# A full-width last query tile, joint first scores, a scale from a sum of squares, and constant matmuls in planned waits

## The chip, the cores and the metric

The kernel runs on one core of one Trainium2 chip. What is measured is the device time of one execution in microseconds (us). The kernel before was run three times; one more execution was taken with a profile.

## The reference

An attention layer with a memory term feeds two dense blocks, one after the other. B = 4 batches, H = 8 heads, S = 576 positions, D = 64; the model width is 512, the hidden width 2048, and there are 2304 tokens. All inputs are f32.

```python
scores = where(causal, -1e9, (q @ k.T) / sqrt(D))
a = exp(scores - scores.max(-1)); a /= a.sum(-1) + 1e-9
local = a @ v
q_p = phi(q)                       # phi(x) = where(x > 0, x, exp(x) - 1) + 1
mem_out = (q_p @ M_prev) / (q_p @ z_prev + 1e-6)
g = sigmoid(beta)                  # one per head
x = g * mem_out + (1 - g) * local  # then [tokens, 512]
h = x @ w_in;  x = (h * sigmoid(h)) @ w_out            # first layer
h = x @ w_in2; y = (h * tanh(softplus(h))) @ w_out2    # second layer
```

## The kernel before

**Attention.** Heads are worked in 16 pairs, one head on partitions 0 to 63 and one on 64 to 127. Each pair is visited twice (`VISITS`): the first 16 visits do query tiles 0 and 1 (128 queries each), the next 16 do tiles 2, 3 and 4. Tile 4 has only 64 queries, as 576 = 4 x 128 + 64. A step is one tile of one visit (`STEPS`), 80 in all. `stage_a` makes the scores of a step into PSUM, takes the row maximum on VectorE (L580), the exponential on ScalarE, a high and a low f16 half, and transposes both by DMA. `stage_b`, three steps later, multiplies the transposed halves with V and the memory matrices, and divides. `stage_c` transposes the result on TensorE (L645) and stores it.

The scores of tiles 0 and 1 contract over 64 rows, one head at a time, in f32, each tile as an operation of its own: four records on 64 rows, then two mask matmuls on 128. For tile 4 both heads stand side by side as 128 columns of a block-diagonal operand (`q4s`, high and low); the products with V take 64 of those columns for each head, into PSUM partitions 0 to 63, so their stationary operand is 128 x 64, and the following transpose works on 64 rows.

**The two layers.** Tokens are worked in nine chunks of 256 (`TOK`), first all chunks through layer one, then through layer two. `gemm1` and `gemm2` are the matmuls, on f16 halves; the second layer does them by a scheme of seven products. `chunk_x` loads a chunk, finds a power of two to scale it by, and makes the halves. The scale comes from `largest`: the row maxima go onto a diagonal (`diag`), an f32 matmul with a constant spreads them over all partitions, and VectorE takes the maximum. `weight_scale` uses `largest` too, twice for each layer. The first layer's weights are put together from two 32-bit words on ScalarE and VectorE while they are loaded (`weight_unit`, VectorE's share at L357); the second layer's are read during attention, put together and written back (`weight_single`, to `wd`), and read again later (`weight_pair`).

**The order.** Everything is handed to a planner (`Plan`) with a priority, a choice of engines, an estimated duration, and the regions it writes and reads. `issue` then plays the work through against these estimates, engine by engine, and emits each instruction at its place; each engine runs its instructions in that order. Attention's priorities grow by `A_RATE` = 2.3 a step, so attention and the first layer's matmuls share TensorE. Until a planned time of 50 us (`COLD`) the estimates of TensorE are doubled. In `mm` a matmul's estimate comes from its columns, its type and its rows.

All operations go through a few helpers, so many rows carry a helper's line: L409 every matmul, L349 every activation, L354, L357 and L363 VectorE's tensor-scalar, scalar-tensor-tensor and tensor-tensor (L363 GpSimd's too), L419 every plain DMA.

Of the kernel before, what the change touches and what calls it, by code (L numbers as in the profile page):

```python
# [9 lines left out]
F32 = mybir.dt.float32  # L10
# [24 lines left out]
COLD = 50000.  # L35
XMAX = 8.0
WMAX = ((128.0, 2048.0), (4.0, 64.0))
# [21 lines left out]
class Plan:  # L59
# [6 lines left out]
    def __init__(self):  # L66
        self.ops, self.seen, self.shared = [], {}, set()

    @staticmethod
    def region(a):  # L70
        if isinstance(a, tuple):
            return a
        ap = a.ap
        size = SIZE[a.dtype]
        p0, f0 = divmod(a.offset, ap[0][0])
        f1 = f0 + sum(st * (n - 1) for st, n in ap[1:]) + 1
        name = a.tensor.name
        return (name, p0, p0 + ap[0][1], f0 * size, f1 * size)

    def add(self, prio, choices, writes, reads, tail=0, edge=(0, 0), shared=False):  # L80


        k, deps = len(self.ops), set()
        for regs, w in ((reads, False), (writes, True)):
            for r in map(self.region, regs):
# [12 lines left out]
        if shared:  # L98
            self.shared.add(k)
        return k  # L100
# [4 lines left out]
    def issue(self):  # L105
# [10 lines left out]
        moved, stream = 0.0, 0.0  # L116
# [13 lines left out]
        for _ in range(n):  # L130
# [56 lines left out]
def attn_moe_moe2_kernel(ctx: ExitStack, tc: tile.TileContext, kq, vm, beta, w1, w2, out):  # L187
# [45 lines left out]
    gb, = buf("gb", [H], F32)  # L233
    gv, = buf("gv", [H // 2, 4], F32)
    eps, = buf("eps", [4], F32)
# [27 lines left out]
    diagr, mxr = ring(buf("diag", [128], F32, 2)), ring(buf("mx", [4], F32, 4))  # L263
# [9 lines left out]
    arenas = {F32R: buf("arena_r", [3584], F32R)[0], F32: buf("arena", [18432], F32)[0]}  # L273
# [23 lines left out]
    q1r, q2r, q4s = ring(carve([256], F32, 2)), ring(carve([2, 256], F32R, 2)), carve([2, D], F32R, 2)  # L297
# [3 lines left out]
    scr, topr, scaler, gvr = ring(scales), ring(carve([2], BF16, 3)), ring(carve([1], F32, 3)), ring(carve([4], F32, 3))  # L301
    er_ = ring(carve([S], F32, 2))
    pr, phr = ring(carve([1024], F32, 2)), ring(carve([16, 128], F16, 3))
# [93 lines left out]
    def mm(prio, ms, whole=False):  # L397

        ns, edge = 0, None
        for o, l, r, _, _ in ms:  # L400
            n = cols(o)
            load, more = (107, 58) if r.dtype == F32 else (107, 42) if r.dtype == F32R else (14, 2.5)
            one = max((2 if r.dtype == F32 else 1) * n / 2.4 * l.shape[0] / 128 + more, 30)
            ns += one
            edge = (edge or (load, 0))[0], one

        def go():
            for o, l, r, a, z in ms:
                nc.tensor.matmul(out=o, lhsT=l, rhs=r, start=a, stop=z)  # L409

        writes = [m[0] for m in ms]
        if whole:
            writes = [(t, 0, 128, b0 // 2048 * 2048, -(-b1 // 2048) * 2048) for t, _, _, b0, b1 in map(plan.region, writes)]
        plan.add(prio, [("PE", ns, go)], writes, [x for m in ms for x in m[1:3]], edge=edge)
# [13 lines left out]
    def setup():  # L428
        p = -1e9
        other(p, "SP", 100, lambda: nc.scalar.dma_start(out=gb, in_=beta), [gb])  # L430
        for x, t in enumerate(q4s):
            for r, e in ((slice(0, 64), 1), (slice(64, 128), 0)):
                o = t[r, e].bitcast(F32)
                plan.add(p + x, [
                    ("DVE", 0.52 * cols(o) + 68, lambda o=o: nc.vector.memset(o, 0.0)),
                    ("POOL", 1.0 * cols(o) + 60, lambda o=o: nc.gpsimd.memset(o, 0.0))], [t[r]], [])

        def consts():
            make_identity(nc, ident16)
            nc.gpsimd.memset(mask, 0.0)  # L440

            for r, c, n in ((slice(0, 128), 0, 128), (slice(0, 64), 128, D), (slice(64, 128), 128, D)):
                m = mask[r, c:c + n]
                nc.gpsimd.affine_select(
                    out=m, in_=m, compare_op=ALU.is_ge, fill=-1e9, base=0, pattern=[[-1, n]], channel_multiplier=1)
            make_identity(nc, ident)
            nc.gpsimd.memset(eps[:, 0:2], 1e-9 * PSCALE)
            nc.gpsimd.memset(eps[:, 2:4], 1e-6)
            nc.gpsimd.memset(ones, 1.0)
            nc.gpsimd.memset(onesf, 1 / XMAX)  # L450
# [5 lines left out]
        other(p, "POOL", 2000, consts, [ident16, mask, ident, eps, ones, onesf, *scales, *v1s])  # L456
# [28 lines left out]
    def prep_q(v, j, prio):  # L485
# [6 lines left out]
        src, q2 = rq[v][:, 256:512], q2r()  # L492
        qq[v, 1] = q2[:, 0], q2[:, 1]
# [14 lines left out]
    def prep_v(v, prio):  # L508
# [6 lines left out]
        total = bank[7][:, 400:401]  # L515
# [22 lines left out]
    def stage_a(n, sbk, prio):  # L538
# [4 lines left out]
        b0 = 512 * sbk[turn[0] % len(sbk)]  # L543
        turn[0] += 1
        ph, P, m1 = phr(), pr(), mr()
        if qt < 4:

            scs = [banks[:, b0 + 512 * e:b0 + 512 * e + N] for e in range(2)]
            ms, nb = [], 4 * nk
# [8 lines left out]
            masks = [(sc[:, N - 128:N], ident16, mask[:, 0:128], False, True) for sc in scs]  # L558
            mm(prio, [x for y in zip(*ms) for x in y] + masks)
            both = banks[:, b0:b0 + 1024].rearrange("p (e c) -> p e c", e=2)[:, :, 0:N]  # L560
# [40 lines left out]
    def stage_b(n, prio):  # L601

        v, qt = STEPS[n]
        R = min(128, S - 128 * qt)
# [3 lines left out]
        if qt < 4:  # L608
            pw = pts.pop(n).rearrange("p (s e k) q -> p s k e q", s=2, e=2)
        else:  # L610
            pw = pts.pop(n).rearrange("p (s k) (e q) -> p s k e q", s=2, e=2)
        ms = []
        for e in range(2):
            o = vb[0:R, 65 * e:65 * e + 65]
# [6 lines left out]
        mm(prio, ms + [(vb[0:R, 130:260], er[v][:, 128 * qt:128 * qt + R], rm[v], True, True)])  # L621
# [3 lines left out]
        g = banks[0:R, 512 * 6:512 * 8].rearrange("p (b c) -> p b c", b=2)[:, 0:m, 0:260].rearrange("p b (a c) -> p b a c", a=4)  # L625
        den, t4, x = denr()[0:R, 0:m], t4r()[0:R, 0:m], xr()[0:R, 0:m]
        each = lambda y: y[0:R].unsqueeze(1).to_broadcast([R, m, 4])
# [3 lines left out]
        tt(prio, t4, g[:, :, :, 0:D], den.unsqueeze(3).to_broadcast([R, m, 4, D]), ALU.mult)  # L631
        tt(prio, x, t4[:, :, 0:2], t4[:, :, 2:4], ALU.add, ("POOL", "DVE"))
        xts[n] = (x, R)

    def stage_c(n, prio):
# [5 lines left out]
        x, R = xts.pop(n)  # L641
        m = 1 + qt % 2
        for i in range(m):
            x2, o = x[:, i].rearrange("p e d -> p (e d)"), bank[6 + i][:, 260:260 + R]
            plan.add(prio, [("PE", 131, lambda o=o, x2=x2: nc.tensor.transpose(o, x2, ident[0:R, 0:R]))], [o], [x2, ident],  # L645
                     edge=(107, 56))
        b, hp = divmod(p, H // 2)
        if b == 0 and qt < 2:
# [4 lines left out]
        copy(prio, xo.rearrange("p (b c) -> p b c", b=m),  # L653
             banks[:, 512 * 6:512 * 8].rearrange("p (b c) -> p b c", b=2)[:, 0:m, 260:260 + R])
# [4 lines left out]
    def largest(prio, s, top, spot, root=0.0):  # L659
# [7 lines left out]
        o = spot[:, 384:512]  # L667
        mm(prio, [(o, onesf, d, True, True)])
        reduce(prio, m, o, ALU.max, AX)
# [106 lines left out]
    def chunk_x(l, c, prio, spot):  # L776
        r, sc, x, top = xs0, xsc(), (xsets, x7r)[l](), mxr()[:, 0:1]
# [3 lines left out]
        if (l, c) != (0, 0):  # L781
            dma(prio, r, src[:, t0:t0 + TOK].rearrange("(k p) t -> p k t", p=128), reads=[(name, 0, NC, t0, t0 + TOK)])
        reduce(prio, top, r, ALU.max, mybir.AxisListType.XY, True)
        largest(prio, s, top, spot)
# [197 lines left out]
    def inputs(l, c, prio):  # L982

        nonlocal n_att
        if l == 0:
# [5 lines left out]
            for u in range(NU * (c - 1) // TOPS, min(NU, NU * c // TOPS)) if c else ():  # L991
                weight_single(u, att_prio(12 + 3.5 * u))
                if u % (NU // 2) == NU // 2 - 1:
                    weight_scale(1, u // (NU // 2), MOE, bank[7])
        xs_of[l, c] = chunk_x(l, c, prio, bank[0] if (l, c) == (0, 0) else bank[7])
# [87 lines left out]
```

## Time and profile before

| what | us |
|---|---|
| three runs, median | 955.02 |
| lowest and highest of them | 950.59, 956.07 |
| profiled execution, whole time | 952.23 |
| its span (first to last instruction) | 950.1 |
| TensorE busy in it | 905.0 |
| VectorE, ScalarE, GpSimd busy | 726.8, 616.4, 400.1 |

The span is what the trace covers; the whole time of that execution is 2.1 us more. Times in the trace count from the start of the span. A busy engine is one with an instruction in flight; matmuls overlap each other, so their price is read from the distance between starts, not from their durations. In the trace an f32 matmul that takes two passes stands as two records.

### The profile page before, as it was taken

Reading aid. Unit: us, or ns where it says so; the run is one execution under the profiler, and the core shown is the slowest. Engines: PE = TensorE matmul, PEld = TensorE weight load, DVE = VectorE, ACT = ScalarE, POOL = GpSimd, SP = SyncE. Lnnn points to the kernel's source line nnn. Section 1 sums busy time; section 2 is a strip of 40 time slices with the busy share of each in tenths; the row PEclk is TensorE's granted clock in tenths of the full one; section 3 lists DMA queues with packets and bytes.
Section 4 is the critical chain, followed back from the end, with each engine's and each line's share of the span. In section 5 each row is a group of like instructions: output and inputs, shape, how many; then the busy total and the mean of one; then the engine's idle time right before and its main releaser. Section 6 shows DMA issues by size and latency. Waiting matters only on the chain.

```text
span 950.1 us, 25452 instructions
## 1 busy us (share of the span) xinstructions
PE 905.0 (95%) x10436; PEld 796.3 (84%) x10436; DVE 726.8 (76%) x1532; ACT 616.4 (65%) x1075; POOL 400.1 (42%) x574
## 2 busy tenths in 40 slices
PE   4569899999999999999999999999999999999997
PEld 3448688888788788788888888999999999999996
DVE  5697876787887877878769756767887888878875
ACT  6889978897787776766655555554555545555553
POOL 1103302342433254324236758254554636635552
PEclk9759899999999999999999999999999999999999
DMA  8978879899699498397453253510010010010010
GB/s 257 316 194 251 193 210 231 257 269 255 177 270 260 139 251 196 85 210 164 101 140 122 90 201 111 178 46 23 25 46 24 23 47 23 25 46 13 13 24 23
DMA packets 155155, 131.29 MB, mean 138 GB/s; under 512 B 111776, under 2 KB 138912, under 8 KB 150944
## 3 DMA queue, kind: packets, MB, share of 16 engines
q1 hardware_dynamic: 154896, 129.68, 51.9%
q8 instruction: 81, 1.33, 0.6%
q14 instruction: 34, 0.28, 0.1%
q10 hardware_dynamic: 144, 0.00, 0.0%
HBM read 77.75 MB, written 25.69 MB: 109 GB/s over the span
## 4 chain that ended last, share of the span: by engine, by line
PE 55%; DVE 1%; ACT 1%; issue 1%; DMA 0%; POOL 0%; ACTq 0%; DVEq 0%
PE banks L409 55%; DVE arena L357 0%; ACT arena L349 0%; PE banks L645 0%; DVE ws L357 0%; ACT w L349 0%; DVE arena L363 0%; DMA yd<-w 0%; POOL g L363 0%; DVE diag L354 0%; DVE mx L366 0%; ACT g L349 0%; ACT ga L349 0%; DVE ga L357 0%; DVE w L357 0%
## 5 line engine op out<-in xcount | busy, mean ns | idle before, releaser
L409 PEld LDWEIGHTS <-w 128*128 128x128 f16 (+1 forms) x3584 | 344.8, 99 | 70.3 <-DVE w L357 23.4
L409 PE MATMUL banks<-arena 128*128 128x128 f16 (+6 forms) x4752 | 292.8, 222 | 6.2 <-ACT arena L349 4.5
L409 PEld LDWEIGHTS <-arena 128*128 128x128 f16 (+1 forms) x4464 | 231.8, 100 | 9.0 <-issue 4.6
L409 PE MATMUL banks<-xh,w 128*128 128x256 f16 x1728 | 210.9, 274 | 4.4 <-DVE xh L357 2.8
L409 PE MATMUL banks<-g,w 128*128 128x256 f16 x1728 | 209.7, 273 | 2.7 <-DVE w L357 1.4
L409 PE MATMUL banks<-w,g 128*128 128x256 f16 x1512 | 181.7, 273 | 0.0
L409 PEld LDWEIGHTS <-g 128*128 128x128 f16 x1512 | 143.9, 98 | 15.2 <-DVE g L357 0.2
L363 POOL TENSOR_TENSOR g<-ga,g 128x512 f16<-128x512 f32 x72 | 98.5, 1371 | 112.3 <-ACT g L349 108.0
L357 DVE SCALAR_TENSOR_TENSOR arena<-arena 128x256 f16<-128x256 f32 (+6 forms) x144 | 112.5, 789 | 11.2 <-ACT arena L349 11.0
L363 POOL TENSOR_TENSOR arena<-arena 128x256 f32<-128x256 f32 x72 | 64.8, 907 | 132.7 <-DVE arena L363 113.1
L349 ACT ACTIVATE arena<-arena 128x256 f32<-128x256 f32 (+6 forms) x184 | 105.0, 593 | 20.6 <-PE banks L409 15.8
L363 POOL TENSOR_TENSOR xh<-xh 128x128 f32<-128x128 f32 x142 | 72.7, 532 | 87.7 <-ACT xh L349 85.8
L363 POOL TENSOR_TENSOR w<-w 128x128 f32<-128x128 f32 x144 | 79.7, 575 | 64.5 <-ACT w L349 62.4
L349 ACT ACTIVATE arena<-banks,arena 128x128 f32<-128x128 f32 (+4 forms) x144 | 73.7, 546 | 32.0 <-DVE arena L580 23.8
L580 DVE TENSOR_REDUCE arena<-banks 128x2 f32<-128x256 f32 (+3 forms) x80 | 64.2, 803 | 24.9 <-PE banks L409 22.1
L349 ACT ACTIVATE ga<-banks,xsc 128x512 f32<-128x512 f32 x72 | 49.4, 686 | 48.7 <-PE banks L409 48.2
L349 ACT ACTIVATE w<-banks 128x128 f32<-128x128 f32 x72 | 19.7, 273 | 82.3 <-PE banks L409 82.3
L357 DVE SCALAR_TENSOR_TENSOR ga<-ga,banks 128x512 f32<-128x512 f32 x72 | 49.0, 680 | 28.2 <-ACT ga L349 27.8
L357 DVE SCALAR_TENSOR_TENSOR g<-w,xsc,g 128x384 f16<-128x384 f32 (+1 forms) x72 | 54.9, 770 | 17.2 <-ACT g L349 16.8
L357 DVE SCALAR_TENSOR_TENSOR g<-xh,xsc,g 128x384 f16<-128x384 f32 (+1 forms) x72 | 56.4, 786 | 10.1 <-ACT g L349 9.1
L349 ACT ACTIVATE g<-ga 128x512 f16<-128x512 f32 x72 | 45.2, 628 | 18.6 <-DVE ga L357 18.2
L349 ACT ACTIVATE g<-w,xsc 128x384 f16<-128x384 f32 (+1 forms) x72 | 46.5, 661 | 8.5 <-POOL w L363 8.0
(117 smaller groups left out, 1108.6 us busy)
## 6 DMA issues: line engine op xcount, KB each, us to landing
ws<-w SPq DMA_DIRECT2D x22, 1024.0 KB, 6.7
arena<-kq SPq DMA_DIRECT2D x16, 576.0 KB, 4.8
w<-w SPq DMA_DIRECT2D x8, 1024.0 KB, 7.7
wd<-w SPq DMA_DIRECT2D x16, 512.0 KB, 3.9
arena<-vm SPq DMA_DIRECT2D x16, 325.0 KB, 4.0
yd<-w SPq DMA_DIRECT2D x36, 128.0 KB, 3.3
ws<-wd SPq DMA_DIRECT2D x9, 512.0 KB, 3.9
xs<-yd SPq DMA_DIRECT2D x9, 512.0 KB, 3.8
```

The lines of the kernel that those rows point to most:

```text
L349: return ("ACT", ns, lambda: nc.scalar.activation(out=out, in_=in_, func=func, scale=scale, bias=bias))
L357: return ("DVE", 1.04 * cols(out) + 160 - over[0], lambda: nc.vector.scalar_tensor_tensor(out=out, in0=in0, scalar=s, in1=in1, op0=op0, op ...
L363: return (e, ns, lambda: eng.tensor_tensor(out=out, in0=in0, in1=in1, op=op))
L409: nc.tensor.matmul(out=o, lhsT=l, rhs=r, start=a, stop=z)
L580: other(prio, "DVE", 1.04 * cols(both) + 70, lambda: nc.vector.tensor_reduce(out=m1, in_=both, axis=AX, op=ALU.max, negate=True), [m1], [b ...
```

## The change

- **Last query tile.** The queries of tile 4 are scaled with those of tiles 2 and 3 and then copied into two masked halves: `own` holds 1 on the partitions of a head and 0 elsewhere. In `stage_b` the products with V take all 128 columns (both heads) for each head's V, into 128 partitions; a masked phi (`e4r`) and a masked gate (`g4`) cancel the halves that belong to the other head. The transpose becomes 128 x 128, and the two 64-column halves of its result are added. The masked copies, the phi, the gate and the sum may go to GpSimd or VectorE.
- **Joint first scores.** Step 0 of a visit makes the scores of tiles 0 and 1 in one TensorE operation, into one pair of banks: tile 0 in columns 0 to 127, tile 1 in columns 128 to 383. All 64-row matmuls come first, then all four masks. Step 1 makes no scores of its own.
- **Scale from a sum of squares.** In `chunk_x` the squares of the row maxima (bf16) are summed over the partitions by one bf16 matmul with ones, one column; the scale is a power of two near `XNORM` over the root of the sum. `weight_scale` of the second layer keeps the diagonal, in two halves in banks 6 and 7.
- **Planner.** New estimates for f32 and two-pass matmuls and for partial rows or columns, and 94 ns for each change of array shape. `regions` tells strided accesses apart where one region covered them before. After a planned time of 70 us (`FILL_FROM`), each time in which the plan has TensorE waiting is filled to six tenths with matmuls of constants, one for each 28 ns, into 60 unused columns of bank 7.
- **Smaller.** `weight_single` gets the priority of 12 attention steps later. The clearing of `q4s` is gone, small buffers moved.

```diff
     def issue(self):
...
-                    ns += max(0, self.ops[k][4][0] - stream)
-                    stream = self.ops[k][4][1]
+                    edge = self.ops[k][4]
+                    ns += max(0, edge[0] - stream) + 94 * (edge[2] != kind)
+                    stream, kind = edge[1], edge[3]
+                    if t > FILL_FROM:
+                        for _ in range(int((t - busy) * FILL_PART / FILL_NS)):
+                            self.fill()
+                    busy = t + ns
...
+        plan.fill = lambda: nc.tensor.matmul(out=bank[7][:, 452:512], lhsT=ident16, rhs=mask[:, 0:60], start=True, stop=True)
...
-        for e in range(2):
-            r = slice(64 * e, 64 * e + 64)
-            src, hi, lo = rq[v][r, 512:576], q4s[0][r, e], q4s[1][r, e]
-            copy(prio, hi, src, 0.125)
-            stt(prio, lo, src, 0.125, hi, ALU.mult, ALU.subtract)
+        for i in range(2):
+            tt(prio, q4s[i], q2[:, i, 256:320].bitcast(F32).unsqueeze(1).to_broadcast([128, 2, D]),
+               own[:, 0:2].unsqueeze(2).to_broadcast([128, 2, D]), ALU.mult, ("POOL", "DVE"))
...
-                if qt < 2:
-                    ms.append([(sc, qq[v, 0][r, c], rk[v][r, 0:N], True, False)])
-                else:
+                if qt == 0:
+                    late = banks[:, b0 + 512 * e + 128:b0 + 512 * e + 384]
+                    ms.append([(sc, qq[v, 0][r, 0:128], rk[v][r, 0:128], True, False),
+                               (late, qq[v, 0][r, 128:256], rk[v][r, 0:256], False, False)])
+                    masks = masks + [late]
+                elif qt > 1:
...
-            pw = pts.pop(n).rearrange("p (s k) (e q) -> p s k e q", s=2, e=2)
+            pw = pts.pop(n).rearrange("p (s k) q -> p s k q", s=2).unsqueeze(3).to_broadcast([128, 2, nk, 2, 128])
...
-        mm(prio, ms + [(vb[0:R, 130:260], er[v][:, 128 * qt:128 * qt + R], rm[v], True, True)])
+        if qt < 4:
+            f = er[v][:, 128 * qt:128 * qt + 128]
+        else:
+            f, g4 = e4r(), gvr()
+            tt(prio, f.rearrange("p (e q) -> p e q", e=2), er[v][:, 512:576].unsqueeze(1).to_broadcast([128, 2, D]),
+               own[:, 0:2].unsqueeze(2).to_broadcast([128, 2, D]), ALU.mult, ("POOL", "DVE"))
+            tt(prio, g4, gvv, own, ALU.mult, ("POOL", "DVE"))
+            gvv = g4
+        mm(prio, ms + [(vb[:, 130:260], f, rm[v], True, True)])
...
+            xw = xwr()
+            copy(prio, xw, bank[6][:, 260:388])
+            tt(prio, xo, xw[:, 0:R], xw[:, R:2 * R], ALU.add, ("POOL", "DVE"))
...
-        largest(prio, s, top, spot)
+        tt(prio, t16, top, top, ALU.mult)
+        mm(prio, [(spot, ones, t16, True, True)])
+        ts(prio, p, spot, 1e-36, ALU.max)
+        inverse(prio, s, p)
+        ts(prio, s.bitcast(U32), s.bitcast(U32), 1, ALU.logical_shift_right, 0x7F800000, ALU.bitwise_and)
+        ts(prio, s, s, 2.0**64 * XNORM, ALU.mult)
...
-                weight_single(u, att_prio(12 + 3.5 * u))
+                weight_single(u, att_prio(24 + 3.5 * u))
```

## Rows read from the trace of the kernel before

**Rows 1.** The chain that ended last: start us, us, what.

```profile
582.49 360.87 PE banks L409 x4774
```

**Rows 2.** Busy us of each engine by stretch, instructions, clock, DMA share, GB/s.

```profile
core 0: us, PE busy (x) PEld busy (x) DVE busy (x) ACT busy (x) POOL busy (x), PEclk, DMA share, GB/s
0.00:75.00 75.00, 44.51 (x327) 31.55 (x328) 52.09 (x125) 58.59 (x103) 9.61 (x33) 0.77 0.91 258
...
100.00:110.00 10.00, 7.50 (x48) 4.73 (x45) 8.07 (x26) 8.08 (x17) 1.47 (x3) 0.66 1.19 237
110.00:300.00 190.00, 187.68 (x1979) 157.96 (x1980) 149.98 (x306) 154.31 (x278) 61.98 (x63) 1.00 0.94 232
300.00:500.00 200.00, 197.18 (x2284) 166.36 (x2281) 154.60 (x308) 137.44 (x246) 75.65 (x88) 1.00 0.70 167
500.00:600.00 100.00, 99.37 (x913) 88.65 (x911) 70.54 (x77) 56.69 (x67) 66.62 (x64) 1.00 0.42 140
600.00:943.00 343.00, 343.00 (x4615) 324.78 (x4613) 266.89 (x647) 177.01 (x324) 173.23 (x314) 1.00 0.10 33
```

**Rows 3.** Timeline of TensorE, 100 to 112 us; in brackets the idle time before.

```profile
103.80 1.03 PE L409 MATMUL banks<-w 128*128 128x128 bf16 x8 [1.99 <-DVE w L357]
...
110.93 1.05 PE L409 MATMUL banks<-g,w 128*128 128x256 f16 x8 [1.36 <-DVE w L357]
```

**Rows 4.** Timeline of TensorE, 111 to 117 us; neighbours alike in names are merged.

```profile
111.92 0.65 PE L409 MATMUL banks<-arena 128*128 128x65 f16 x8
112.41 0.27 PE L645 MATMUL banks<-ident,arena 128*128 128x128 f32 x1
112.52 2.46 PE L409 MATMUL banks<-g,w 128*128 128x256 f16 x21
114.81 0.83 PE L409 MATMUL banks<-arena 128*128 128x65 f16 x14
115.47 1.15 PE L409 MATMUL banks<-g,w 128*128 128x256 f16 x9
116.55 0.49 PE L409 MATMUL banks<-arena 64*128 64x128 f32 x4
```

**Rows 5.** Timeline of TensorE, 300 to 324 us.

```profile
300.39 1.15 PE L409 MATMUL banks<-xh,w 128*128 128x256 f16 x9
301.47 1.39 PE L409 MATMUL banks<-arena 128*64 128x65 f16 x32
302.79 2.79 PE L409 MATMUL banks<-xh,w 128*128 128x256 f16 x24
...
320.05 0.39 PE L409 MATMUL banks<-diag,onesf 128*128 128x128 f32 x2
320.28 0.82 PE L409 MATMUL banks<-g,w 128*128 128x256 f16 x6
320.93 0.17 PE L409 MATMUL banks<-arena,ones 128*128 128x1 bf16 x1
320.96 0.49 PE L409 MATMUL banks<-g,w 128*128 128x256 f16 x3
...
322.72 0.27 PE L645 MATMUL banks<-ident,arena 64*128 64x64 f32 x1 [0.16 <-ACT arena L349]
322.93 1.16 PE L409 MATMUL banks<-g,w 128*128 128x256 f16 x9
```

**Rows 6.** TensorE's groups by form from 110 us on: busy us, mean ns.

```profile
L409 PE MATMUL banks<-diag,onesf 128*128 128x128 f32 x38 | 7.4, 278 | 0.2 <-DVE diag L354 0.2
...
L409 PE MATMUL banks<-arena 64*128 64x128 f32 x24 | 3.0, 322 | 0.0
```

**Rows 7.** DMA issues on the tile `wd`: duration ns, first and last start us.

```profile
L419 SPq DMA_DIRECT2D wd<-w x16: 319/386/1107, 126.5 to 353.6; - x16
...
L419 SPq DMA_DIRECT2D arena<-wd x7: 319/320/402, 484.6 to 580.6; - x7
```

**Rows 8.** Timeline of VectorE, 441 to 450 us.

```profile
444.73 1.37 DVE L363 TENSOR_TENSOR arena<-arena 128x8 f32<-128x8 f32 x1
```

**Rows 9.** Timeline of GpSimd, 441 to 450 us.

```profile
444.01 2.07 POOL L363 TENSOR_TENSOR arena_r<-arena,arena_r 128x576 fp32r<-128x576 f32 x1 [1.71 <-ACT arena_r L349]
```

More of the change, by code (lines that the diff above doesn't have):

```diff
@@ L66, in __init__, with regions @@
     def __init__(self):
-        self.ops, self.seen, self.shared = [], {}, set()
+        self.ops, self.seen, self.shared, self.fill = [], {}, set(), None
     @staticmethod
-    def region(a):
+    def regions(a):
         if isinstance(a, tuple):
-            return a
+            return [a]
         ap = a.ap
@@ L75, in region, with add @@
         p0, f0 = divmod(a.offset, ap[0][0])
[L76 to L80, printed above, removed]
+        (step, count), inner = ap[1], 1 + sum(st * (n - 1) for st, n in ap[2:])
+        if count > 4 or inner >= step:
+            step, count, inner = 0, 1, inner + step * (count - 1)
+        return [(a.tensor.name, p0, p0 + ap[0][1], (f0 + step * i) * size, (f0 + step * i + inner) * size) for i in range(count)]
+    def add(self, prio, choices, writes, reads, tail=0, edge=(0, 0, (False, False), (False, False)), shared=False):
         k, deps = len(self.ops), set()
         for regs, w in ((reads, False), (writes, True)):
-            for r in map(self.region, regs):
+            for r in [y for x in regs for y in self.regions(x)]:
                 log = self.seen.setdefault(r[0], [])
@@ L115, in issue @@
         at, on, end = [0.0] * n, [None] * n, [0.0] * n
-        moved, stream = 0.0, 0.0
+        moved, stream, kind, busy = 0.0, 0.0, (False, False), 0.0
         port = {"DVE": 0.0, "POOL": 0.0}
@@ L269, in attn_moe_moe2_kernel @@
     gram = [bank[i][:, 0:128] for i in range(2)]
-    arenas = {F32R: buf("arena_r", [3584], F32R)[0], F32: buf("arena", [18432], F32)[0]}
+    arenas = {F32R: buf("arena_r", [3840], F32R)[0], F32: buf("arena", [18432], F32)[0]}
     pos = dict.fromkeys(arenas, 0)
@@ L300, in attn_moe_moe2_kernel @@
     scales = carve([4], F32, 3)
-    scr, topr, scaler, gvr = ring(scales), ring(carve([2], BF16, 3)), ring(carve([1], F32, 3)), ring(carve([4], F32, 3))
+    scr, topr, scaler, gvr = ring(scales), ring(carve([2], BF16, 3)), ring(carve([1], F32, 3)), ring(carve([4], F32, 4))
     er_ = ring(carve([S], F32, 2))
+    (gb,), (gv,), (eps,) = carve([H], F32), carve([H // 2, 4], F32), carve([4], F32)
+    own, e4r, xwr = carve([4], F32)[0], ring(carve([128], F32, 2)), ring(carve([128], F32, 2))
     pr, phr = ring(carve([1024], F32, 2)), ring(carve([16, 128], F16, 3))
@@ L397, in mm @@
     def mm(prio, ms, whole=False):
-        ns, edge = 0, None
+        ns, edge, kind = 0, None, None
         for o, l, r, _, _ in ms:
-            n = cols(o)
-            load, more = (107, 58) if r.dtype == F32 else (107, 42) if r.dtype == F32R else (14, 2.5)
-            one = max((2 if r.dtype == F32 else 1) * n / 2.4 * l.shape[0] / 128 + more, 30)
+            n, half = cols(o), l.shape[0] < 128
+            if r.dtype == F32:
+                load, one = 107, 2 * max(n / 1.2 * (0.5 if half else 1) + 3, 55 if half else 111)
+            elif r.dtype == F32R:
+                load, one = 107, n / 4.8 + 6 if half else n / 2.4 + 48
+            else:
+                load, one = 14, max(n / 2.4 * (0.5 if half else 1) + 2.5, 29)
+            now = half, cols(l) < 128
+            if kind not in (None, now):
+                ns += 94
+            kind = now
             ns += one
-            edge = (edge or (load, 0))[0], one
+            edge = (*(edge or (load, 0, now))[0:1], one, *(edge or (load, 0, now))[2:3], now)
         def go():
@@ L412, in mm @@
         if whole:
-            writes = [(t, 0, 128, b0 // 2048 * 2048, -(-b1 // 2048) * 2048) for t, _, _, b0, b1 in map(plan.region, writes)]
+            writes = [(t, 0, 128, b0 // 2048 * 2048, -(-b1 // 2048) * 2048) for x in writes for t, _, _, b0, b1 in plan.regions(x)]
         plan.add(prio, [("PE", ns, go)], writes, [x for m in ms for x in m[1:3]], edge=edge)
@@ L449, in consts @@
             nc.gpsimd.memset(ones, 1.0)
+            nc.gpsimd.memset(own, 0.0)
+            for e in range(2):
+                nc.gpsimd.memset(own[64 * e:64 * e + 64, e:4:2], 1.0)
             nc.gpsimd.memset(onesf, 1 / XMAX)
@@ L454, in consts @@
                 nc.gpsimd.memset(t[:, :, :, D:D + 1], 1.0)
-        other(p, "POOL", 2000, consts, [ident16, mask, ident, eps, ones, onesf, *scales, *v1s])
+        plan.fill = lambda: nc.tensor.matmul(out=bank[7][:, 452:512], lhsT=ident16, rhs=mask[:, 0:60], start=True, stop=True)
+        other(p, "POOL", 2000, consts, [ident16, mask, ident, eps, ones, onesf, own, *scales, *v1s])
         act(p, gb, gb, AF.Tanh, 0.5)
@@ L557, in stage_a @@
                                (sc, ql[r, c], kh[r, 0:N], False, False)])
-            masks = [(sc[:, N - 128:N], ident16, mask[:, 0:128], False, True) for sc in scs]
-            mm(prio, [x for y in zip(*ms) for x in y] + masks)
-            both = banks[:, b0:b0 + 1024].rearrange("p (e c) -> p e c", e=2)[:, :, 0:N]
+            masks = [(sc[:, cols(sc) - 128:], ident16, mask[:, 0:128], False, qt > 1 or i > 1) for i, sc in enumerate(masks)]
+            if qt != 1:
+                mm(prio, [x for y in zip(*ms) for x in y] + masks)
+            both = bass.AP(scs[0].tensor, scs[0].offset, [scs[0].ap[0], [512, 2], [1, N]])
             P = P[:, 0:2 * N].rearrange("p (e c) -> p e c", e=2)
@@ L624, in stage_b @@
         m = 1 + qt % 2
-        g = banks[0:R, 512 * 6:512 * 8].rearrange("p (b c) -> p b c", b=2)[:, 0:m, 0:260].rearrange("p b (a c) -> p b a c", a=4)
-        den, t4, x = denr()[0:R, 0:m], t4r()[0:R, 0:m], xr()[0:R, 0:m]
-        each = lambda y: y[0:R].unsqueeze(1).to_broadcast([R, m, 4])
+        g = banks[:, 512 * 6:512 * 8].rearrange("p (b c) -> p b c", b=2)[:, 0:m, 0:260].rearrange("p b (a c) -> p b a c", a=4)
+        den, t4, x = denr()[:, 0:m], t4r()[:, 0:m], xr()[:, 0:m]
+        each = lambda y: y.unsqueeze(1).to_broadcast([128, m, 4])
         tt(prio, den, g[:, :, :, D], each(eps), ALU.add)
@@ L640, in stage_c @@
         p = VISITS[v][0]
-        x, R = xts.pop(n)
-        m = 1 + qt % 2
+        x, m, R = xts.pop(n), 1 + qt % 2, min(128, S - 128 * qt)
         for i in range(m):
-            x2, o = x[:, i].rearrange("p e d -> p (e d)"), bank[6 + i][:, 260:260 + R]
-            plan.add(prio, [("PE", 131, lambda o=o, x2=x2: nc.tensor.transpose(o, x2, ident[0:R, 0:R]))], [o], [x2, ident],
-                     edge=(107, 56))
+            x2, o = x[:, i].rearrange("p e d -> p (e d)"), bank[6 + i][:, 260:388]
+            plan.add(prio, [("PE", 109, lambda o=o, x2=x2: nc.tensor.transpose(o, x2, ident))], [o], [x2, ident],
+                     edge=(107, 109, (False, False), (False, False)))
         b, hp = divmod(p, H // 2)
@@ L666, in largest @@
             ts(prio, d, ident, top, ALU.mult, 1e-30, ALU.max)
-        o = spot[:, 384:512]
-        mm(prio, [(o, onesf, d, True, True)])
-        reduce(prio, m, o, ALU.max, AX)
+        if spot is None:
+            o = banks[:, 512 * 6:512 * 8].rearrange("p (b c) -> p b c", b=2)[:, :, 388:452]
+            mm(prio, [(o[:, i], onesf, d[:, 64 * i:64 * i + 64], True, True) for i in range(2)])
+            reduce(prio, m, o, ALU.max, mybir.AxisListType.XY)
+        else:
+            o = spot[:, 384:512]
+            mm(prio, [(o, onesf, d, True, True)])
+            reduce(prio, m, o, ALU.max, AX)
         inverse(prio, s, m)
```

51 lines of the change are left out of this document (25 added, 26 removed).

## The prediction, made before the change was run

> **What bounds the kernel now.** I read the chain that ended last first: its longest piece is 360.87 us of TensorE matmuls without a wait, which ends at 943 us of a span of 950.1 [rows 1]. Then the stretches [rows 2]. The reader should see three stages there. Up to about 110 us TensorE is not the bound: in 0 to 75 it is busy 44.51 of 75 us, ScalarE 58.59, and the DMA engines run at 0.91; in 100 to 110 it is busy 7.50 of 10 at a granted clock of 0.66, and its two waits of 1.99 and 1.36 us there both end with VectorE's `w L357`, which puts weights together that have come by DMA [rows 3]. From 110 to 600 TensorE is busy 187.68 + 197.18 + 99.37 = 484.2 of 490 us, so all its visible waits are 5.8 us. From 600 to 943 it is busy 343.00 of 343. So work taken off TensorE after 110 us should come off the end, and work taken off before 110 should mostly go into waits for weights. The granted clock is 1.00, that is 2.4 GHz, in every stretch after 110.
>
> **The change part by part.**
>
> Price of a change of array shape. One 256-column f16 matmul takes 2.29/21 = 0.109 us (112.52 to 114.81) [rows 4]. Nine of them ahead of a 64-row score take 1.08 us (115.47 to 116.55), 0.10 more than 9 x 0.109 [rows 4]; nine ahead of the 64-column products take 1.08 too (300.39 to 301.47) [rows 5]. On the way out it is the same: the narrow transpose holds TensorE 0.21 us (322.72 to 322.93) [rows 5], the full one 0.11 (112.41 to 112.52) [rows 4]. So each entry or exit costs about 0.095 us.
>
> Last query tile at full width. Before, each of the 16 head pairs goes into the 64-column shape and out again for its products with V, and into the 64-row shape and out again for its transpose: 64 switches. A few of these blocks stand beside another partial-array block, so one switch stays; I take 60, at 0.095: 5.7 us. All lie after 110 us, since the last tiles belong to the second half of the visits. The products themselves: the narrow block of 32 records takes 1.32 us with its exit, 1.22 without (301.47 to 302.79) [rows 5]. The full shape: 8 records take 0.49 us (111.92 to 112.41) and 14 take 0.66 (114.81 to 115.47) [rows 4]; both hold the same two f32 records, so six f16 products take 0.17, that is 0.028 each, and the two f32 ones 0.32. Thirty f16 and two f32 ones: 30 x 0.028 + 0.32 = 1.17. Gain 0.05 x 16 = 0.8. The wide transpose costs 0.11, the narrow one 0.21 with its exit already counted: nothing. This part: 6.5 us.
>
> Joint first scores. Tiles 0 and 1 of a visit now go through the 64-row shape together: one entry and one exit fewer, 0.19 us. Only the visits after 110 us count: 24 records at four a visit [rows 6], 6 visits, 1.1 us. The ten earlier ones fall into the stage that waits for weights and get nothing; their cover gone, they would be worth 1.9. The joint operation also keeps one pair of banks for both tiles, so the next tile's scores wait until both were read; with MoE matmuls ready to go in between I cost that at nothing, and at up to one wait like those above if it fails.
>
> Scale from a sum of squares. The f32 matmul over the diagonal holds TensorE 0.23 us (320.05 to 320.28), a one-column bf16 one 0.03 (320.93 to 320.96) [rows 5]: 0.20 saved. After 110 us there are 38/2 = 19 diagonal matmuls [rows 6]; two are weight scales, which keep it, so 17 x 0.20 = 3.4 us, of which nine, 1.8 us, lie in the second layer. VectorE loses a 128-wide diagonal and a 128-wide reduction and gains small ones of one column; the chain to the scale gets shorter if anything. It ends in no visible TensorE wait after 600, so I cost it at nothing.
>
> Work moved to GpSimd. Per last tile: two masked copies of the queries, one masked phi, one masked gate, one sum of two 64-column halves. No row has these shapes on GpSimd; below, nothing, if they lie wholly in its idle time; above, a GpSimd operation of 2.07 us lets VectorE's 128x8 operation beside it take 1.37 us [rows 8, 9], so all of it could be charged to VectorE. GpSimd is busy 61.98 of 190 and 75.65 of 200 us in the two attention stretches, VectorE 149.98 and 154.60 [rows 2]: there is room, and VectorE sheds the four small 64-row pieces. I take nothing; the upper end is a rival. The extra sum delays the tile's store by one small operation, with MoE chunks later than it.
>
> Second-layer weights by 12 steps later. The 16 write-backs run from 126.5 to 353.6 us [rows 7], 15.1 us apart for 3.5 steps of priority, 4.3 us a step: 12 steps are 52 us, so the last comes at about 405. The row of reads into the arena begins at 484.6 [rows 7]. 80 us of slack: nothing; a loss needs the attention steps to slip by that much. It takes some ScalarE work out of 110 to 300, its fullest stretch (154.31 of 190), into 300 to 500 (137.44 of 200): a gain I cannot size, between nothing and part of the 5.8 us of waits.
>
> The fill. Ahead of each wait that the planner sees after its 70 us, it puts one 60-column matmul per 28 ns of six tenths of it. One such matmul must cost about 0.029 us, between the 0.028 of one with 65 columns [rows 4] and the 0.03 of one with a single column [rows 5]. Where the real wait is at least as long it costs nothing; where TensorE had work ready it costs all of it. How much the planner sees is not in the trace: from nothing, up to rival one. If its waits are those seen, 5.8 us, the fill is at most 3.5 us, nearly all inside them. It can give nothing back through the clock after 110 us, since that is at 1.00 already; in 100 to 110, 0.66 means 6.8 us at 1.2 GHz, so at most 3.4 us, in a stage that ends with weights. I take nothing either way. A new order of instructions comes with all this, since the planner's prices change; it can open or close waits of the size seen, 0.2 to 1.4 us each.
>
> Sum: 6.5 + 1.1 + 3.4 = 11.0 us. The profiled execution took 952.2 (span 950.1): 941.2. The median of the three runs is 955.0, 2.8 above it, which would give 944.0. I take 943: between the two, with nothing for the waits.
>
> **The rivals.**
>
> One, slower: the fill goes onto a busy TensorE. After 600 us TensorE has no wait at all, so whatever the planner sees there is paid for. 11.0 us are eaten by 11.0/0.029 = 380 fillers, which by the formula are 380 x 28/0.6 = 17.7 us of planned waits; 0.5% slower needs 15.8/0.029 = 545 fillers, 25 us. A planner that believes in waits of a tenth of those 343 us would put 20.6 us of matmuls there: 961.8. For it: a plan on estimated durations need not know that this stage never waits. Against: 98.8% busy from 110 to 600 means that plan and chip agree fairly well there. 10 in 100.
>
> Two, the same: the gain is not kept where other engines share the stage. From 110 to 600 TensorE sheds 9.2 us, but VectorE, at 78% of 110 to 500, is held by the added GpSimd work as in [rows 8, 9], or the joint scores hold their banks, and waits of the same sum open. Only the nine second-layer scales stay: 950.4, or 953.2 on the median. For it: VectorE's stretched operations. Against: 85 us of idle VectorE time. 15 in 100.
>
> Three, faster still: the new order closes the waits too. All 5.8 us, and 3.4 of clock in 100 to 110, would give 932; half of it 936.6. 20 in 100.
>
> Four, slower: the weight load of the wide tile paces it. If a 128-column load made each of the 480 products take twice its narrow 0.030 us, that adds 14.4 us and takes the 0.8 back: 956.4. Against it stand the wide products at 0.028 [rows 4]. 2 in 100. The Trainium skill (TensorE: Matmul & The Clock Gate, LDWEIGHTS) says that a load's time goes with its columns; by its P/1.2 the wide load would be 53 ns longer, an estimate of 25.6 us over 480 products, were loads not hidden. The trace's 0.028 with 128-column loads speaks against that.
>
> Five, slower: the second layer's weights come late after all, and the first stage of that layer stands for them; from 80 us of slippage on each further us is lost, and 19 of them give 960. 3 in 100.
>
> **How the numbers follow.** The forecast as summed has 50 in 100, its own range 938 to 949. A measurement of this kernel tells about 0.5%, 4.8 us, from no change, so faster means under 950.2. Forecast and rival three are faster: 0.70. Rival two is the same: 0.15. One, four and five: 0.15 slower. The range from 930 to 957 takes in rival three nearly whole and rival two, with the median's offset, and leaves out one, most of five and the far ends.
>
> **What would show it.** In the profile after: no 64-column products and no narrow transposes among TensorE's forms; 0.11 around the transposes of the last tile; 64-row scores in blocks of eight records; one-column matmuls where the diagonal ones were, and two pairs of the latter left. From 600 us on each second-layer chunk should be 0.2 us shorter. Wrong it would be if fillers appear by the hundred in the second layer, if the busy share of 110 to 600 falls under 98%, or if waits for VectorE or GpSimd grow by as much as the switches gave.

## The result, and the profile after

The changed kernel took 938.25 us (median; 937.45 to 939.34), the kernel before 953.5 us in the same comparison: a ratio of 0.9842, with a 95% interval of 0.9808 to 0.9876. The forecast was 943, within 930 to 957. The profiled execution took 938.56 us, its span is 936.8, against 952.23 and 950.1: 13.7 us less in time and 13.3 in span, where the sum had said 11.0.

The busy time of each engine by stretch, after:

```profile
core 0: us, PE busy (x) PEld busy (x) DVE busy (x) ACT busy (x) POOL busy (x), PEclk, DMA share, GB/s
100.00:110.00 10.00, 8.74 (x184) 7.99 (x183) 8.68 (x28) 8.08 (x16) 4.24 (x4) 1.00 0.83 221
110.00:590.00 480.00, 477.48 (x5274) 417.20 (x5272) 364.56 (x668) 340.81 (x566) 248.43 (x292) 1.00 0.75 192
590.00:930.00 340.00, 340.00 (x4599) 321.92 (x4597) 261.62 (x653) 175.30 (x322) 177.04 (x310) 1.00 0.10 32
```

From 110 us to the last stage TensorE's visible waits are 2.5 us, where [rows 2] gave 5.8; the last stage still has none. In 100 to 110 us the granted clock is 1.00 where it was 0.66, and the stage did not end earlier for it, as the next view shows.

The timeline of TensorE after, at the first stage's end, around two score blocks, and at a last tile:

```profile
102.58 1.59 PE L467 MATMUL banks<-mask,ident 128*128 128x60 bf16 x52
...
108.27 1.81 PE L467 MATMUL banks<-mask,ident 128*128 128x60 bf16 x60 [1.26 <-DVE arena L370]
...
111.62 2.46 PE L424 MATMUL banks<-g,w 128*128 128x256 f16 x21
113.91 0.83 PE L424 MATMUL banks<-arena 128*128 128x65 f16 x14
114.57 0.82 PE L424 MATMUL banks<-g,w 128*128 128x256 f16 x6
115.32 0.93 PE L424 MATMUL banks<-arena 64*128 64x128 f32 x8
116.18 0.40 PE L424 MATMUL banks<-mask,ident 128*128 128x128 bf16 x4
...
124.17 0.17 PE L424 MATMUL banks<-mx,ones 128*128 128x1 bf16 x1
124.20 1.03 PE L424 MATMUL banks<-g,w 128*128 128x256 f16 x8
...
272.73 1.37 PE L424 MATMUL banks<-arena 128*128 128x65 f16 x32
273.93 0.49 PE L424 MATMUL banks<-xh,w 128*128 128x256 f16 x3
274.44 0.41 PE L666 MATMUL banks<-ident,arena 128*128 128x128 f32 x2
274.69 0.49 PE L424 MATMUL banks<-xh,w 128*128 128x256 f16 x3
```

The constant matmuls are the rows of L467: 52 and 60 of them stand in the wait for weights (102.58, 108.27). The first layer's second matmuls (`g,w`) begin at 111.62; in the kernel before they went on at 110.93, after a first one [rows 3]. A joint score block holds TensorE for 0.86 us (115.32 to 116.18), and the matmuls ahead of it end 0.10 late once (114.57 + 6 x 0.109 is 115.22). A last tile's products take 1.20 us (272.73 to 273.93) where [rows 5] had 1.32, with no late end ahead of them. The scale's matmul takes 0.03.

The chain that ended last, after; L467 is the fill:

```profile
510.54 0.55 PE banks L467 x20
511.10 34.75 PE banks L424 x325
545.85 0.33 PE banks L467 x12
546.18 108.19 PE banks L424 x1274
654.56 74.25 PE banks L424 x1010
729.03 74.25 PE banks L424 x1010
803.50 74.25 PE banks L424 x1010
877.97 48.67 PE banks L424 x651
926.64 0.47 PE banks L467 x17
```

The fill stands on the path here: 20, 12 and 17 constant matmuls are links of the chain, and the gaps of 0.22 us between its long pieces (654.56 + 74.25 to 729.03) hold seven or eight more each. Its group from 112 us on:

```profile
L467 PE MATMUL banks<-mask,ident 128*128 128x60 bf16 x83 | 3.6, 190 | 0.0
```

An account of starts says where the 13.3 us of the span came from. From the tenth `g,w` matmul on (112.52 us before, 112.60 after; the same matmuls of both layers and the same attention blocks are left, and in e10 one small block more, some 0.7 us) I gave each TensorE matmul the time to the next one's start, so that a wait or a late entry is charged to the matmul ahead of it:

```
us from the tenth g,w on      before   after   without fill   narrow tile   one region
                                               (e2)           (e4)          (e10)
products with V                61.5     58.0    58.0           60.7          59.3
transposes                      9.2      7.3     7.3            9.9           8.3
scores, tiles 0 and 1           6.4      5.1     5.1            5.1           5.1
scores, tiles 2 to 4           42.4     42.6    42.5           42.6          45.2
scales of chunks and weights    4.4      1.4     1.4            1.5           2.3
constant matmuls                0.0      2.3     0.0            3.7           0.0
first layer                   366.4    360.5   360.7          360.6         371.5
second layer                  333.9    333.8   333.8          333.8         333.8
masks, V scales                 7.0      6.9     6.9            7.8           7.4
total                         831.2    817.8   815.8          825.8         833.0
```

The second layer's own matmuls cost the same to 0.2 us. What fell is what the change touches, and the first layer, by 5.9 us: its matmuls stand ahead of the entries (changes into a 64-row or 64-column shape) and of the waits, and are charged with them. The changes of shape themselves fall from 144 to 76: 12 fewer for the scores of tiles 0 and 1, 56 fewer for the last tile.

### The profile page after: what moved, and what is told of

Read it like the earlier page. It is cut to its first block, busy times and chain, and to the rows that moved or that the text cites. A ratio compares the mean times of both kernels' runs of the same rounds, so it can differ in the third digit from the quotient of the medians.

```text
span 936.8 us, 25926 instructions
## 1 busy us (share of the span) xinstructions
PE 891.7 (95%) x10638; PEld 799.3 (85%) x10638; DVE 711.4 (76%) x1520; ACT 605.6 (65%) x1044; POOL 448.6 (48%) x650
## 3 DMA queue, kind: packets, MB, share of 16 engines
q8 instruction: 83, 1.36, 0.6%
## 4 chain that ended last, share of the span: by engine, by line
PE 67%; DVE 1%; ACT 0%; issue 0%; DVEq 0%
PE banks L424 66%; PE banks L666 0%; DVE ws L364 0%; PE banks L467 0%; DVE arena L370 0%; ACT arena L356 0%; DVE arena_r L364 0%; DVE arena L364 0%; DVE arena L523 0%; DVE arena L361 0%; ACT w L736 0%; DVE arena L595 0%; DVE ga L364 0%; ACT ga L356 0%; DVE w L364 0%
## 5 line engine op out<-in xcount | busy, mean ns | idle before, releaser
L424 PE MATMUL banks<-arena 128*128 128x128 f16 (+5 forms) x4752 | 285.9, 221 | 9.1 <-ACT arena L356 8.8
L424 PEld LDWEIGHTS <-arena 128*128 128x128 f16 x4464 | 230.8, 98 | 6.2 <-issue 3.0
L424 PE MATMUL banks<-g,w 128*128 128x256 f16 x1728 | 205.3, 273 | 0.0
L370 POOL TENSOR_TENSOR arena<-arena 128x256 f32<-128x256 f32 (+3 forms) x150 | 102.7, 688 | 183.5 <-DVE arena L370 82.9
L424 PE MATMUL banks<-w,g 128*128 128x256 f16 x1512 | 178.8, 273 | 0.0
L364 DVE SCALAR_TENSOR_TENSOR arena<-arena 128x256 f16<-128x256 f32 (+6 forms) x144 | 109.1, 763 | 11.6 <-ACT arena L356 11.3
L356 ACT ACTIVATE arena<-arena 128x256 f32<-128x256 f32 (+7 forms) x182 | 104.5, 594 | 19.1 <-PE banks L424 15.9
L370 POOL TENSOR_TENSOR xh<-xh 128x128 f32<-128x128 f32 x138 | 76.7, 576 | 54.6 <-ACT xh L356 52.6
L364 DVE SCALAR_TENSOR_TENSOR g<-xh,xsc,g 128x384 f16<-128x384 f32 (+1 forms) x72 | 53.0, 742 | 7.7 <-ACT g L356 7.0
L370 DVE TENSOR_TENSOR arena<-banks,arena 128x8 f32<-128x8 f32 (+1 forms) x96 | 36.2, 377 | 27.7 <-PE banks L424 16.8
```

What stands on the lines that cost most here:

```text
L356: return ("ACT", ns, lambda: nc.scalar.activation(out=out, in_=in_, func=func, scale=scale, bias=bias))
L364: return ("DVE", 1.04 * cols(out) + 160 - over[0], lambda: nc.vector.scalar_tensor_tensor(out=out, in0=in0, scalar=s, in1=in1, op0=op0, op ...
L370: return (e, ns, lambda: eng.tensor_tensor(out=out, in0=in0, in1=in1, op=op))
```

## The experiments

Ratios are to the kernel before, with their 95% interval; times are medians of 4 to 12 runs. The kernel before had medians of 953.3 to 954.7 us in the three sets. The expectations weigh up to three theories. One: the gain is TensorE work that was removed, and the fill only costs. Two: something else sets the pace, as other engines, the new order or, in e9, the longer chain to the scale. Three: the fill pays by holding the clock.

**e1, the changed kernel again.** No edit.

> The changed kernel once more, as the mark for the others of this set. All theories: about 0.984 of the kernel before, 938 us.

938.72 us, 0.9841 (0.9818 to 0.9865), span 936.1. It is the mark for the rest.

**e2, without the fill.**

```diff
-FILL_FROM, FILL_PART, FILL_NS = 70e3, 0.6, 28
+FILL_FROM, FILL_PART, FILL_NS = 1e12, 0.6, 28
```

> The changed kernel without the constant matmuls; the order of all other instructions is the same. Theory one (the gain is TensorE work that was removed, and the fill is only a cost): the 83 constant matmuls after 112 us cost 83 x 0.028 = 2.3 us, mostly where the profile after shows no wait; without them about 936. The 133 before 112 us lie in the wait for weights and change nothing, though the granted clock of 100 to 110 us falls back to about 0.66. Theory three (the fill pays by holding the clock): about 941, three us above the changed kernel.

935.21 us, 0.9805 (0.9781 to 0.9829), span 933.9 against 936.1. In the account every kind of work is the same to 0.2 us, and the 83 constant matmuls' 2.3 us are gone. Theory one holds, though one thing expected did not come: in 100 to 110 us the granted clock is 0.94, not 0.66, as its low stretch lies later, at 0.50 from 109 to 112 us. The first stage's end without the fill:

```profile
108.59 0.54 PE L666 MATMUL banks<-ident,arena 128*128 128x128 f32 x2 [2.70 <-DVE cvec L370]
108.92 1.12 PE L424 MATMUL banks<-arena 128*128 128x65 f16 x8
109.84 3.59 PE L424 MATMUL banks<-g,w 128*128 128x256 f16 x21
113.27 0.83 PE L424 MATMUL banks<-arena 128*128 128x65 f16 x14
```

After 2.70 us without work the 21 matmuls take 3.43 us instead of 2.29; with the fill the granted clock is 1.00 there, so the fill does hold it. But with the fill they begin later, after the 60 constant matmuls. The tenth `g,w` matmul starts at 111.76 here, at 111.99 in e1 and at 112.60 in the first profile of the changed kernel: no gain by the fill is left at this point.

**e3, the shape changes put back, in the same order.**

```diff
+    def narrow():
+        nc.tensor.matmul(out=bank[7][0:64, 452:453], lhsT=ident16[:, 0:64], rhs=mask[:, 0:1], start=True, stop=True)
...
         def go():
+            if ahead is not None:
+                ahead()
             for o, l, r, a, z in ms:
```

`narrow` is called ahead of each last tile's products and its transpose.

> The changed kernel with one constant one-column matmul on 64 columns ahead of each last tile's products and one ahead of its transpose; the planner does not know of them, so the order stays. Each adds an entry and an exit of the 64-column shape, 0.19 us, and itself 0.03; 32 of them 7.0 us. Theory one: all of it shows, about 945. Theory two (other engines set the pace of the attention stage, and the gain came from the new order): under 2 us, at most 940.

945.82 us, 0.9913 (0.9893 to 0.9933): 7.1 us over e1, where 7.0 was worked out, and the account from the tenth `g,w` on grows by 7.3. One of them in the timeline:

```profile
270.64 2.46 PE L429 MATMUL banks<-g,w 128*128 128x256 f16 x21
273.03 0.19 PE L405 MATMUL banks<-mask,ident 128*64 128x1 bf16 x1
273.15 1.38 PE L429 MATMUL banks<-arena 128*128 128x65 f16 x32
```

The 21 matmuls would end their starts at 270.64 + 21 x 0.109 = 272.93; the narrow one starts at 273.03, and the next at 273.15, 0.12 after it. So 0.10 on entry and about 0.09 on exit, and all of it reaches the end: theory two falls for this part. The Trainium skill (TensorEngine Tiling (Array Packing), Key Properties) says that a change of tiling mode drains TensorE; the trace agrees with 0.095 us each way.

**e4, the last tile narrow again** (products and transpose as before the change; the masked queries stay).

```diff
-            pw = pts.pop(n).rearrange("p (s k) q -> p s k q", s=2).unsqueeze(3).to_broadcast([128, 2, nk, 2, 128])
+            pw = pts.pop(n).rearrange("p (s k) (e q) -> p s k e q", s=2, e=2)
...
-            o = vb[:, 65 * e:65 * e + 65]
+            o = vb[0:R, 65 * e:65 * e + 65]
```

> The changed kernel with the last tile's products and transpose back on 64 columns and 64 rows (the masked queries stay as changed). The planner knows and makes a new order. Theory one: 6.5 us more TensorE work, about 944.5, within 2 us for the new order. Theory two: 936 to 940, since the shape does not matter.

946.29 us, 0.9917 (0.9895 to 0.9938): 7.6 us over e1. In the account it is 8.0, of which 1.4 are constant matmuls (132 instead of 83 from the tenth `g,w` on): 6.6 us for the shape, as worked out. It has 58 changes of shape more, which at 0.095 are 5.5; about 1 us of the 6.6 is the products' own and the new order's.

**e5, the diagonal back, without the fill** (halves of 64 columns in the first layer).

```diff
-        tt(prio, t16, top, top, ALU.mult)
-        mm(prio, [(spot, ones, t16, True, True)])
...
+        largest(prio, s, top, spot)
```

> The changed kernel without the constant matmuls and with the scale of each token chunk found again by the diagonal, the f32 matmul and the reduction over 128 columns (in the first layer as two halves of 64 columns). Theory one: 17 such scales after 112 us at 0.2 us of TensorE each, 3.4 us above the kernel without constant matmuls: 938.6, give or take 1.5 for the new order. Theory two: 935 to 936, as the matmul lies beside others' waits in the attention stage, and at most 1.8 us of it shows, those of the second layer.

942.71 us, 0.9875 (0.9858 to 0.9892): 0.7% over e2, some 6.7 us, more than either theory expected. The edit was itself dearer than the diagonal of before, since a half costs nearly as much as a whole:

```profile
125.63 0.56 PE L424 MATMUL banks<-diag,onesf 128*128 128x64 f32 x4
126.02 0.49 PE L424 MATMUL banks<-g,w 128*128 128x256 f16 x3
```

The four records of two halves take 0.39 us, the two of a whole 0.23 [rows 5]. The account has 4.9 us more for scales. Hence e9.

**e6, the first scores apart again.**

```diff
-        if qt != 1:
-            turn[0] += 1
-        b0 = 512 * sbk[turn[0] % len(sbk)] + 128 * (qt == 1)
+        turn[0] += 1
+        b0 = 512 * sbk[turn[0] % len(sbk)]
...
-            if qt != 1:
-                mm(prio, [x for y in zip(*ms) for x in y] + masks)
+            mm(prio, [x for y in zip(*ms) for x in y] + masks)
```

> The changed kernel with the scores of tiles 0 and 1 as two operations again, each from the first column of its own banks. Theory one: by the account of starts after 112 us the six joint blocks there saved 1.2 us in the 64-row matmuls and 0.6 us in entries, so 1.8 us above the changed kernel: 940.5. Theory two: the joint operation pays by making the second tile's scores early; then the row maxima of the stage up to 170 us come later and more than 3 us are lost, 942 or more.

942.79 us, 0.9876 (0.986 to 0.9893): 0.35% over e1's ratio, 3.3 us. The account is 4.4 us longer: the scores' own starts are 1.2 of it, the fill 0.5, and more is charged to masks (1.4) and products (1.9), with 0.7 less in the first layer. These are entries and waits; the visible waits grew by 1.3. That is nearer to theory two's 942, but a new order alone can move as much (e9), so the split is open.

**e7, the second layer's weights 12 steps earlier again.**

```diff
-                weight_single(u, att_prio(24 + 3.5 * u))
+                weight_single(u, att_prio(12 + 3.5 * u))
```

> The changed kernel with the second layer's weights put together 12 steps earlier again. If the later place closed the waits of the attention stage (its visible waits went from 5.8 to 2.5 us from 110 us to the end of that stage), they open again: 941 to 942. If the prices of the planner closed them, or plain chance of the order: within 1.5 us of 938.7.

937.14 us, 0.9815 (0.9797 to 0.9834), no slower than e1. The later place is not needed for the closed waits.

**e8, the planner's old prices**, and none for a change of shape.

```diff
-            if r.dtype == F32:
-                load, one = 107, 2 * max(n / 1.2 * (0.5 if half else 1) + 3, 55 if half else 111)
...
+            load, more = (107, 58) if r.dtype == F32 else (107, 42) if r.dtype == F32R else (14, 2.5)
+            one = max((2 if r.dtype == F32 else 1) * n / 2.4 * l.shape[0] / 128 + more, 30)
```

> The changed kernel with the planner's old prices of TensorE's work and no price for a change of array shape. If true prices closed the waits: 941 to 942, with more constant matmuls or more waits in the trace from 112 us on. If not: within 1.5 us of 938.7.

937.78 us, 0.9826 (0.9806 to 0.9845), also no slower. The truer prices are not needed either. Undoing both at once was not tried.

**e9, the diagonal whole, without the fill.** As e5, with `bank[7]` as the place in the first layer.

> As the run with the diagonal back and no constant matmuls, but with one 128-column matmul per scale in the first layer too, as in the kernel before. The run with halves had four records of 0.1 us per scale there, so it added 4.9 us of TensorE work after 112 us instead of 3.4. Theory one: 3.4 us above the kernel without constant matmuls, about 938.5. Theory two (the longer chain to the scale costs by itself, beside TensorE's work): as with halves, 941 to 943.

944.0 us, 0.9903 (0.9885 to 0.9922): a miss for both theories, 9.3 us over e2's ratio. The scales' own starts are 3.2 us more, as theory one says. The span is 7.9 us longer; 4.4 of it lies in the account from the tenth `g,w` on, the rest ahead:

```profile
100.00:110.00 10.00, 5.37 (x58) 4.14 (x56) 8.46 (x27) 7.61 (x19) 3.21 (x4) 0.89 0.67 187
110.00:200.00 90.00, 88.59 (x904) 74.93 (x904) 72.75 (x155) 73.31 (x142) 31.30 (x36) 0.97 0.82 212
```

TensorE has 4.6 us of waits in 100 to 110 and the clock stays down into the next stretch; its visible waits from 110 to 600 are 4.0 us, 2.1 in e2. The tenth `g,w` comes at 115.26, 3.5 later than in e2, with some attention work done sooner. Whether the longer chain to the scale or just the other order made these waits is not told apart.

**e10, one region for a strided access, without the fill.**

```diff
-        (step, count), inner = ap[1], 1 + sum(st * (n - 1) for st, n in ap[2:])
...
+        f1 = f0 + sum(st * (n - 1) for st, n in ap[1:]) + 1
+        return [(a.tensor.name, p0, p0 + ap[0][1], f0 * size, f1 * size)]
```

> The kernel without constant matmuls with one region for a strided access again, as in the kernel before; all other parts as changed. Its plan differs in that reads of two banks cover the columns between them. If the finer regions closed the waits of the attention stage: 937 to 940, and 2 to 4 us more of visible waits from 110 us to the stage's end. If not: within 1.5 us of 935.2.

950.72 us, 0.9973 (0.996 to 0.9987): nearly all of the gain is gone. Busy time from 110 to 600 us, and its largest wait (TensorE's timeline, then VectorE's):

```profile
110.00:600.00 490.00, 476.98 (x5151) 413.47 (x5149) 368.97 (x663) 335.60 (x563) 244.68 (x290) 0.99 0.74 185
```

```profile
542.30 5.10 PE L422 MATMUL banks<-xh,w 128*128 128x256 f16 x30 [2.16 <-DVE ga L362]
547.24 2.02 PE L422 MATMUL banks<-g,w 128*128 128x256 f16 x17
```

```profile
539.02 2.63 DVE L362 SCALAR_TENSOR_TENSOR arena<-arena,wsc 128x1792 f16<-128x1792 f32 x1
541.57 1.27 DVE L362 SCALAR_TENSOR_TENSOR ga<-ga,banks 128x512 f32<-128x512 f32 x2
```

13.0 us of waits. In the largest, two operations that TensorE needs stand behind a 2.63 us weight split on VectorE; and after 2.16 us without work the next 30 matmuls take 4.94 us instead of 3.27, so a wait is paid again as clock (granted 0.66 from 542.3 to 545.6). The account has the first layer's matmuls at 371.5 instead of 360.7. So the finer regions carry the change: with the new tiles, score places and the old regions a plan comes out that waits. Which of the added dependencies does it was not tried.

**e11, e2 and e7 together.**

> The two undone parts that made the changed kernel faster, together: no constant matmuls, and the second layer's weights at the old 12 steps. Without the 127 constant matmuls after 112 us of that order (3.6 us of starts): 933.5. If the earlier place is chance: 935.2 as without constant matmuls alone.

934.32 us, 0.98 (0.9777 to 0.9823), span 935.1 against 933.9 in e2. Not to be told from e2: without the fill the earlier weights show no gain. Both beat the changed kernel by 0.4%.

**e12, the kernel before with the fill alone** (same code as in the change, in `bank[6]`, between 70 and 480 us of the plan).

> The kernel before with the fill alone, in bank 6 and from 70 to 480 us of the plan, its order unchanged. Theory one: the clock of 100 to 110 us rises from 0.66, but the stage ends with weights and the fill takes TensorE's time, so 0 to 3 us slower: 954 to 957. Theory three: 951, faster by the 3.4 us that the lower clock could cost there.

951.83 us, 0.9987 (0.9975 to 0.9998): 0.1% or 1.2 us faster, between 0.2 and 2.4. Theory one, which had 0 to 3 us slower, misses; the time is near theory three's 951, but the 3.4 us that it stands for lie outside the interval. The clock of 100 to 110 us did rise:

```profile
100.00:110.00 10.00, 8.66 (x180) 6.92 (x178) 8.58 (x27) 8.61 (x19) 2.40 (x3) 1.00 0.98 233
```

The tenth `g,w` starts at 112.29 instead of 112.52, and the span of its profiled execution is 950.5, 950.1 before, so the two traces do not show where the 1.2 us lie.

## Why the prediction came out right, and where its terms were off

The mechanism held: TensorE bounds the kernel after 110 us, and what was taken off it came off the end. That the sum came within 3 us is in part luck: the waits and the fill were both put at nothing, and their errors partly cancel.

**TensorE's work after 110 us.** This step held. Work put back came back: 7.1 us for 7.0 in e3, in an unchanged order. The last tile was worked out at 6.5 us and e4 measures 6.6 apart from its fill. Its parts were less exact: 56 changes of shape went, not 60, and the products save 0.02 us a tile (1.22 without the exit, now 1.20), not 0.05, which together make 5.6. The wide products also settle rival four: the 128-column load does not pace them.

**Joint first scores.** Mis-sized: 1.1 us was worked out from entries and exits. In the account the six blocks' own starts fall by 1.2, and six entries ahead of them, 0.6, come on top: 1.8. A joint block's own starts are 0.2 us shorter than the two apart (0.86 for 0.42 + 0.64). One exit is 0.1 of it; the other 0.1 stands at tile 1's first pair of records, which holds TensorE 0.32 us at the head of a block of its own and 0.22 inside the joint one. The term left this out. The undo (e6) does not confirm the size.

**Squares.** 3.1 us for 3.4: the two weight scales, now in halves, cost more than before.

**Work before 110 us.** Rightly costed at nothing: the tenth `g,w` matmul starts at 112.60 for 112.52, and at 111.99 in e1.

**The fill.** The one term that failed in kind: costed at nothing, it costs 2.3 us from 112 us on, since 80 of its 83 matmuls stand from 510 us on, where TensorE does not wait. That is rival one's mechanism at a ninth of its price: in the second layer the 0.22 us of fill in a chunk take back the 0.2 that its scale gave. Its clock gain in 100 to 110 us was also put at nothing. That came out for the changed kernel, though by another way: the fill holds the clock and spends the gain itself (e2). The most that shows anywhere is the 1.2 us of e12.

**The waits.** Costed at nothing, and they gave some 4.3 us: 13.4 in the account, less 6.5, 1.8 and 3.1, plus the fill's 2.3. Counted by themselves they give nearly that: the matmuls ahead of a visible wait overrun their usual distance by 7.2 us before and 3.2 after. The visible part is 5.8 to 2.5 us from 110 us on. This is rival three by about half, and with the fill against it the sum came out 2.7 short. Neither the place of the weights (e7) nor the prices (e8) is needed for it, each undone alone; e10 shows that the finer regions are needed for it, though not that they would have closed the waits of the kernel before.

**Rival two.** It did not come: GpSimd's added work is there (248 us busy in 110 to 590, 201 before), VectorE has its room, and the waits fell. But e10 shows how near it lay. With the old regions 2.6 us of the gain are left, where rival two left 1.8. The cause is another: dependencies that the coarse regions add, and the order that follows from them. Of the 13.0 us of waits only 2.9 end with GpSimd, 4.4 with VectorE and 5.3 with ScalarE.

## What to carry to other kernels

Where one engine is busy without a gap to the end, price an edit by the distance between starts on it, and count the changes of array shape: 0.095 us for each entry and exit adds up over dozens of small blocks. To prove such a price, put the cost back without telling the planner, as in e3; an undo that makes a new order can move the time by several us of its own (e9: 9.3 us for 3.2 us of work). And if buffers are packed closer, see first that the dependency tracking can tell them apart: e10 lost 15 us to that.

## What the runs showed of the hardware

An f32 matmul of 64 columns costs nearly what one of 128 does (two of them, four records, 0.39 us; one of 128, two records, 0.23). After 2.16 us without work TensorE took 4.94 us for 30 matmuls of 256 columns, 1.67 more than at their usual 0.109 (e10), as if some 15 of them had run at the lower of the two clock levels, 1.2 GHz; the granted clock is 0.66 from 542.3 to 545.6. After 1.36 us, in the kernel before, eight and a transpose took 0.99 us, the full rate, at a granted 1.00 [rows 3, 4].
